# Dilated attention rows by way of DRAM, dilated tiles first in every batch, and a first batch whose low-rank product is formed in fp32

## The chip, the cores and the metric

The kernel runs on one core of a Trainium2 chip. The metric is the device time of one execution in microseconds (us), the median of several runs; smaller is better. A profiled execution has a time of its own and a span, from its first to its last instruction, and the trace gives each instruction's start and length within that span. The engines are named as in the profile: PE multiplies matrices (PEld loads its weights), DVE, ACT and POOL work on rows of elements, SP issues the transfers (SPq).

## The reference, cut to what matters

Eight batches of 576 tokens. Eight heads of width 64: the first four attend to a window of the last 32 tokens, the last four to 32 tokens spread over 128, every fourth one (dilation 4). The heads side by side give x, 576 x 512 for each batch. Then, with U (576 x 32) and V (32 x 576),

```
mask_plain = (rel >= 0) & (rel < 32)
mask_dil   = (rel >= 0) & (rel < 128) & (rel % 4 == 0)
attn = softmax(where(mask, q @ k.T / 8, -1e9))       # per head
x  = heads side by side of (attn @ v)                # (8, 576, 512)
u  = x + (x.T @ U @ V).T                             # mixes tokens, per batch
out = u + relu(u @ w_ch1) @ w_ch2                    # 512 -> 2048 -> 512
```

U, V and the two weight matrices arrive as 64-bit floating point; everything else is fp32. Below, t is U.T @ x (32 x 512 for a batch), so that V.T @ t is what is added to x.

## The kernel before, in words

**Chunks.** The 4608 tokens are 36 tiles of 128; three tiles make a chunk, and the last loop runs over twelve chunks. In a chunk, `layer1(f)` (L778) multiplies the turned rows of u by 128 columns of w_ch1 in twelve matmuls, for f from 0 to 15; ACT (L783) and DVE (L784) apply the relu and split the result into a high and a low part; `layer2(f)` (L798) multiplies by 128 rows of w_ch2 in nine matmuls. Matrices are split into a high and a low part of a rounded format (fp32r), and three products of parts stand for one fp32 product; an fp32 matmul stands in the profile as two instructions. The attention of later batches is laid into the chunks by a queue with positions, so PE works on both.

**Attention.** A batch has 18 tiles of 64 queries, nine of each kind; two tiles make a group, and there are nine groups (`NGB`). `TILES` gives their order: before, the nine plain tiles and then the dilated ones. For dilated heads the tokens are sorted by their remainder modulo 4, so that a dilated tile is 64 neighbours in that order. A group is scored (L395), masked and reduced (DVE L415), put through exp (ACT L419), turned (PE L432, copied by L434 or L436), multiplied by v (L461, tile pv) and divided by its sum (L465, L466, L489). Plain rows land in their x tile at once (L489). Dilated rows land in a tile xp, and SP copies them from there to every fourth row of x (L493), in as many transfers as `runs_of` finds.

**t and its use.** `split` (L507, L509) makes a high and a low part of half a tile's columns (c is 0 for the plain half, 1 for the dilated half); `t_mm` (L529) multiplies both by U, itself split into parts; `t_evict` (L538 to L544) takes t out of PSUM as four stacked parts of 32 rows, some by ACT and some by DVE. For most tiles `mix` (L553, L555) adds V.T @ t to x. For the three tiles of chunk 0 it is done while they are turned: `lay_x` (L563) turns x by a matmul with the identity and leaves the sum open, `lay_mix` (L570) adds the second term, `transp` (L611 on ACT, L612 on DVE) takes high and low part out. The first batch computes t of its dilated half from xp, before the rows have moved, with rows of U in that order (`us_d`).

**Weights.** Each of the 32 pieces of the two weight matrices (512 KB of 64-bit numbers) and the three pieces of U and V goes through `weight_step`, a pipeline of four stages: `fetch64` on SP (L208, L210), `narrow_a` on ACT (L217 to L219), `narrow_b` with a shift on DVE (L225) and an add on POOL (L226), and for weights `narrow_c`: the high part by ACT (L230) or DVE (L232), the low part by POOL or, for some, DVE (L233). One step advances each stage by a piece. Before, steps for U and V follow items 5 to 10 of the first batch's list, steps for the weights every third item from the eleventh (at a low priority), five more follow the list, and chunk 0 has four per f. Instructions are put in order on each engine by a scheduler that goes by priority and estimated times.

Of the kernel before, what the change touches and what calls it, by code (L numbers as in the profile page):

```python
# [10 lines left out]
F32 = mybir.dt.float32  # L11
# [37 lines left out]
TILES = [(0, j) for j in range(NJ)] + [(1, NJ - 1)] + [(1, j) for j in range(NJ - 1)]  # L49
# [6 lines left out]
PRE_AT = range(5, 11)  # L56
U_AT = 5
PRE_N = 5
W_FROM = 11
W_EACH = 3  # L60
# [4 lines left out]
XL_LAST = 3  # L65
XL_DVE = ((0, 1), (1, 1))
# [18 lines left out]
XHLS = 10  # L85
HI1 = 0.85
POST0 = 0
# [7 lines left out]
XPS = 4  # L95
# [37 lines left out]


def runs_of(b, half, j):
    out = []
    for r in range(QB):
        g = b * S + token_of(half, QB * j + r)
        t, row = divmod(g, P)
        step = 1 if half == 0 else DIL  # L140
        if out and out[-1][1] == t and row == out[-1][2] + step * out[-1][3]:
            out[-1][3] += 1
        else:
            out.append([r, t, row, 1])
    return out
# [14 lines left out]
def attention_moe_kernel(ctx: ExitStack, tc: tile.TileContext, qk1, qk2, vv, masks, wide, ident, ut, vt, w1, w2, out):  # L160
# [28 lines left out]
    signs = [const.tile([P, DM, 2], F16, name=f"sign{i}") for i in range(NSIGN)]  # L189
    NPT = 2  # L190
# [51 lines left out]
    def finish_small(kind):  # L242
        def go(v):
            if kind == "u":
                v3 = v.rearrange("p (a r) -> p a r", r=RANK)
                for dst, src in ((us, v3[:, 0:9]), (held_u[0], v3[:, 9:])):
                    nc.scalar.copy(out=dst[:, :, 0:RANK], in_=src)
                    nc.vector.tensor_tensor(out=dst[:, :, RANK:], in0=src, in1=dst[:, :, 0:RANK].bitcast(F32), op=ALU.subtract)
            else:
                cs = slice(kind * HALF_V, (kind + 1) * HALF_V)  # L250
                nc.scalar.copy(out=vs[:, cs], in_=v)
                lo = slice(3 * RANK, 4 * RANK)
                nc.vector.tensor_tensor(out=vs[lo, cs], in0=v[lo], in1=vs[lo, cs].bitcast(F32), op=ALU.subtract)
        return go

    def finish_w(f, layer, n):
        def go(v):
# [3 lines left out]
            narrow_c(v, h, l, nc.vector if n % L_ON_DVE == 0 and n >= L_FROM else nc.gpsimd, n % 4 < H_ON_ACT)  # L261
# [13 lines left out]
    def weight_step(lo, hi):  # L275
# [10 lines left out]
        if lo <= i - 1 < hi:  # L286
            n = pieces[i - 1][1]
            if 2 * F_LAST <= i - 1 - NSMALL:
# [161 lines left out]

    def weighted(g, pt):
# [5 lines left out]
        for u in range(2):  # L457
            for h in range(2):
                hs = slice(h * DV, (h + 1) * DV)
                for i in range(2):  # L460
                    nc.tensor.matmul(pv[rows[i]:rows[i] + QB, 2 * u + h, :], lhsT=pt[:, 2 * i + u, QB * h:QB * (h + 1)],  # L461
# [8 lines left out]
        for (half, j), row in zip(tiles, rows):  # L470
            if half == 0:
                dst = x_tile((b * S + j * QB) // P)[:, 0:HALF_D]
            else:
# [9 lines left out]
                moves += [(t, to, n, row + r) for r, t, to, n in runs_of(b, half, j)]  # L483
# [8 lines left out]
        for t, to, n, r in sorted(moves):  # L492
            nc.sync.dma_start(out=x_tile(t)[to:to + DIL * (n - 1) + 1:DIL, HALF_D:], in_=xp[r:r + n])  # L493
        if moves and b == 0:
            split(b, part, 1, xp, slice(QB * (2 - len(DPART[part])), P))

    t_ps = {}
    t_sb = {}
    xs = {}

    def split(b, i, c, x, rs):
        if b == 0:
            xhl = early.tile([P, 2, HALF_D], F32R, tag="xhl", name=f"xhl{b}_{i}_{c}", bufs=XHLS)
        else:
            xhl = xpool.tile([P, 2, HALF_D], F32R, tag="x", name=f"xhl{b}_{i}_{c}")
        xh, xl = xhl[:, 0], xhl[:, 1]
        nc.scalar.copy(out=xh[rs], in_=x[rs])  # L507
        eng = nc.vector if (b, c) in XL_DVE or (b == 0 and i >= XL_LAST) else nc.gpsimd
# [6 lines left out]

    def t_mm(b, i, c):
        assert 0 in finished
        parts = batch_parts(b)
        if b == 0 and c == 1:
            u = held_u[0][:, i]  # L520
            rs = slice(QB * (2 - len(DPART[i])), P)
        else:
            t, row, n, tok = parts[i]
            rs = slice(row, row + n)
            u = us[:, 8 if n < P else tok // P if tok % P == 0 else 4 + tok // P]
        if (b, c) not in t_ps:
            t_ps[b, c] = psum.tile([2 * RANK, HALF_D], F32, tag="ps", name=f"t{b}_{c}")
        for k, m in enumerate(xs.pop((b, i, c))):
            nc.tensor.matmul(  # L529
                t_ps[b, c], lhsT=u[rs], rhs=m[rs],  # L530
                start=(i == 0 and k == 0), stop=(i == len(parts) - 1 and k == 1),
            )

    def t_evict(b, c):
        ts_ = work.tile([P, HALF_D], F32R, tag="t" if b else "t0", name=f"ts{b}_{c}", bufs=1 if b else 2)
# [3 lines left out]
        nc.vector.tensor_tensor(out=ts_[r[1]], in0=tp[r[0]], in1=ts_[r[0]].bitcast(F32), op=ALU.subtract)  # L539
        if b == 0:  # L540
            nc.vector.tensor_copy(out=ts_[r[2]], in_=tp[r[1]])
        else:
            nc.scalar.copy(out=ts_[r[2]], in_=tp[r[1]])
        nc.scalar.copy(out=ts_[r[3]], in_=tp[r[0]])  # L544
# [15 lines left out]
    def lay_x(t):  # L560
        tp = psum.tile([P, KC, P], F32, tag="acc", name=f"tp{t}", bufs=CT)
        for k in range(KC):
            nc.tensor.matmul(tp[:, k, :], lhsT=x_tile(t)[:, k * P:(k + 1) * P], rhs=id_sb, start=(k == 0), stop=False)  # L563
        sums[t] = tp

    def lay_mix(t):
        tp = sums.pop(t)
        for k in range(KC):
            c, o = divmod(k, KC // 2)
            nc.tensor.matmul(tp[:, k, :], lhsT=t_sb[0, c][:, o * P:(o + 1) * P],  # L570
                             rhs=vs[:, 64 + t * P:64 + (t + 1) * P], start=False, stop=(k == KC - 1))
        return tp
# [20 lines left out]
    def transp(t):  # L593
# [7 lines left out]
        elif t in sums:  # L601
            tp = lay_mix(t)
# [9 lines left out]
        nc.vector.tensor_tensor(out=l, in0=tp, in1=h.bitcast(F32), op=ALU.subtract)  # L612

    def batch_items(b):
# [3 lines left out]
        for s in range(NGB + LAG):  # L618
# [31 lines left out]
            if b < SPLIT:  # L650
                attn.append([lambda pre=pre, units=units, post=post: (pre(), [x() for x in units], post())])
# [4 lines left out]
        for c in range(2):  # L656
            more = []
            for i in range(n + 1):
                def go(i=i, c=c):
                    if i > 0 and (b, c) != (0, 0):  # L660
                        t_mm(b, i - 1, c)
                    if i < n and (b, c) != (0, 1):
# [5 lines left out]
        first = NJ // 2 + LAG + 1 + (POST0 if b == 0 else 0)  # L668
# [13 lines left out]
        if b == 0:  # L682
            hold = after[0][n + 1:]
# [220 lines left out]
```

## Time and profile before

| | |
|---|---|
| median of 3 runs | 1010.58 us (1010.44 to 1010.71) |
| the profiled execution | 1010.63 us |
| its span | 1008.9 us |
| mean granted clock of PE | 0.987 |
| PE busy | 982.8 us |
| first `layer1` matmul of chunk 0 | 52.96 us |
| first stores of chunk 0 | 148.72 us |
| first `layer1` matmul of chunk 1 | 155.52 us |

A row of a view by groups gives line, engine, operation, output and inputs, shapes and count, then the busy time, the mean of one in ns, and the idle time of the engine ahead of them with what ended it. A row of the timeline gives start, length, engine, line and operation, and in brackets the idle time ahead and its releaser; neighbours of one form are merged. A row of the windows gives for a stretch of time the length, each engine's busy time with its instruction count, the granted clock of PE (1.00 is full), and the busy share and rate of the DMA engines. A busy PE may still run at a reduced clock.

### The profile page before, as it was taken

How to read it: one execution, taken by the hardware profiler on the slowest of the kernel's cores; microseconds unless marked ns; L12 is line 12 of the kernel's file. 1: busy time of each engine (PE TensorE's matmuls, PEld its weight loads, DVE VectorE, ACT ScalarE, POOL GpSimd, SP SyncE). 2: the span in 40 equal slices, each digit the busy share in tenths (PEclk: the TensorE clock that was granted, in tenths of full speed). 3: DMA queues.
4: the chain of work that ended last, by engine and by line, in shares of the span. 5: the costliest groups of instructions: out<-in, count | busy, mean ns of one | idle time of the engine just before them, and what ended most of it. 6: DMA issues, size and time to landing. Idle time of an engine off the chain costs nothing.

```text
span 1008.9 us, 18032 instructions
## 1 busy us (share of the span) xinstructions
PE 982.8 (97%) x5928; PEld 861.8 (85%) x5928; DVE 580.9 (58%) x1957; ACT 408.7 (41%) x985; POOL 326.9 (32%) x520
## 2 busy tenths in 40 slices
PE   6799989999999999999999999999999999999998
PEld 6688768888988889888888888888898888999997
DVE  3878787665468636676367653876547863311211
ACT  5799954443245423344244432444323542111110
POOL 0489954242135413252132430434222431000000
PEclk9699998999999999999999999999999999999999
DMA  9699534332324315243242333433232420500000
GB/s 276 182 302 313 152 111 116 88 113 82 87 78 125 94 38 145 74 121 89 67 115 77 103 91 73 124 89 111 83 87 80 122 63 24 134 1 1 32 1 32
DMA packets 96909, 103.31 MB, mean 102 GB/s; under 512 B 12816, under 2 KB 83536, under 8 KB 96816
## 3 DMA queue, kind: packets, MB, share of 16 engines
q1 hardware_dynamic: 96816, 102.16, 35.6%
q8 instruction: 48, 0.79, 0.3%
q14 instruction: 45, 0.37, 0.1%
HBM read 80.08 MB, written 17.30 MB: 97 GB/s over the span
## 4 chain that ended last, share of the span: by engine, by line
PE 86%; DVE 4%; DMA 2%; ACT 2%; POOL 2%; issue 1%; SPq 1%; DVEq 0%; ACTq 0%; POOLq 0%
PE ph L778 37%; PE acc L798 37%; PE pv L461 4%; PE s L384 3%; PE t L529 2%; PE s L395 2%; POOL v L226 1%; DMA zd<-z 1%; DMA raw<-w 1%; PE m L553 1%; DVE xhl L509 1%; PE ptp L432 1%; ACT sign L218 1%; DMA qk<-qk 1%; ACT sign L219 0%
## 5 line engine op out<-in xcount | busy, mean ns | idle before, releaser
L798 PE MATMUL acc<-w2h,hh 128*128 128x512 f32 x576 | 229.3, 398 | 3.5 <-ACT hh L783 2.2
L798 PE MATMUL acc<-w2l,hh 128*128 128x512 f32 x576 | 228.0, 396 | 0.0
L361 POOL TENSOR_TENSOR qks<-qkr,qks 128x160 fp32r<-128x160 f32 x192 | 103.2, 537 | 375.3 <-ACT qks L360 251.6
L784 DVE SCALAR_TENSOR_TENSOR hl<-ph,hh 128x384 fp32r<-128x384 f32 x192 | 106.2, 553 | 192.2 <-ACT hh L783 191.3
L798 PE MATMUL acc<-w2h,hl 128*128 128x512 f32 x576 | 211.9, 398 | 0.4 <-DVE hl L784 0.4
L783 ACT ACTIVATE hh<-ph 128x384 fp32r<-128x384 f32 x192 | 93.2, 485 | 277.1 <-PE ph L778 267.9
L778 PE MATMUL ph<-uth,w1l 128*128 128x384 f32 x768 | 175.0, 340 | 0.0
L778 PE MATMUL ph<-uth,w1h 128*128 128x384 f32 x768 | 174.6, 342 | 0.3 <-ACT uth L611 0.3
L778 PE MATMUL ph<-utl,w1h 128*128 128x384 f32 x768 | 172.6, 338 | 0.0
L419 ACT ACTIVATE p<-p,nmax 128x160 f32<-128x160 f32 (+1 forms) x288 | 110.3, 408 | 110.3 <-DVE nmax L415 109.0
L778 PEld LDWEIGHTS ph<-uth,w1h 128*128 128x128 f32 x768 | 138.7, 189 | 15.6 <-ACT uth L611 0.5
L778 PEld LDWEIGHTS ph<-uth,w1l 128*128 128x128 f32 x768 | 136.4, 189 | 1.2 <-issue 0.2
L778 PEld LDWEIGHTS ph<-utl,w1h 128*128 128x128 f32 x768 | 135.3, 188 | 1.6 <-DVE utl L612 0.2
L360 ACT CAST qks<-qkr 128x288 fp32r<-128x288 f32 x192 | 80.8, 429 | 121.8 <-PE s L384 81.4
L798 PEld LDWEIGHTS acc<-w2h,hl 128*128 128x128 f32 x576 | 107.4, 188 | 24.4 <-DVE hl L784 1.0
L798 PEld LDWEIGHTS acc<-w2h,hh 128*128 128x128 f32 x576 | 108.2, 188 | 21.2 <-ACT hh L783 3.2
L445 DVE STREAM_TRANSPOSE pt<-p 32x128 f32<-32x128 f32 x384 | 115.6, 301 | 16.7 <-ACT p L419 11.9
L798 PEld LDWEIGHTS acc<-w2l,hh 128*128 128x128 f32 x576 | 108.3, 188 | 16.1
L412 DVE TENSOR_TENSOR p<-s,wide_sb 128x160 f32<-128x160 f32 x192 | 60.0, 318 | 67.7 <-PE s L384 65.8
L364 POOL TENSOR_TENSOR qks<-qkr,qks 64x128 fp32r<-64x128 f32 x192 | 89.1, 464 | 15.0
L509 POOL TENSOR_TENSOR xhl<-x,xhl 128x256 fp32r<-128x256 f32 (+1 forms) x68 | 50.2, 759 | 83.8 <-ACT xhl L507 59.8
L384 PE MATMUL s<-qks 128*128 128x320 f32 x192 | 60.4, 320 | 2.6 <-DVE x L555 1.5
(75 smaller groups left out, 929.2 us busy)
## 6 DMA issues: line engine op xcount, KB each, us to landing
qkr<-qk SPq DMA_DIRECT2D x192, 144.0 KB, 2.2
raw<-w SPq DMA_DIRECT2D x26, 512.0 KB, 5.0
v<-vv SPq DMA_DIRECT2D x126, 97.5 KB, 2.1
out<-x SPq DMA_DIRECT2D x36, 256.0 KB, 2.3
zd<-z SPq DMA_DIRECT2D x120, 64.0 KB, 2.0
xt<-zd SPq DMA_DIRECT2D x30, 256.0 KB, 2.9
qk<-qk SPq DMA_DIRECT2D x9, 448.0 KB, 8.7
qkr<-qk SPq DMA_DIRECT2D x18, 224.0 KB, 4.9
```

The lines of the kernel that those rows point to most:

```text
L360: nc.scalar.copy(out=t[:, 0:QK2], in_=raw)
L361: nc.gpsimd.tensor_tensor(out=t[:, QK2:], in0=raw[:, P:], in1=t[:, P:QK2].bitcast(F32), op=ALU.subtract)
L364: eng.tensor_tensor(out=t[lo, 0:P], in0=raw[lo, 0:P], in1=t[lo, 0:P].bitcast(F32), op=ALU.subtract)
L384: nc.tensor.matmul(sp, lhsT=t[:, 0:P], rhs=t[:, P:], start=True, stop=True)
L412: nc.vector.tensor_tensor(out=p_sb[:, u, :], in0=sp[:, 0:KW], in1=wide_sb[:, kind], op=ALU.add)
L419: nc.scalar.activation(out=p_sb[:, u, 0:w], in_=p_sb[:, u, 0:w], func=AF.Exp, bias=nmax[:, u:u + 1], scale=-1.0,)
L445: nc.vector.transpose(out=to[:, :, WIN * (r % 2):WIN * (r % 2 + 1)], in_=p_sb[rs, :, QB * s + WIN * k:QB * s + WIN * (k + 1)])
L509: eng.tensor_tensor(out=xl[rs], in0=x[rs], in1=xh[rs].bitcast(F32), op=ALU.subtract)
L778: nc.tensor.matmul(ph, lhsT=w[:, k, :], rhs=u[:, k, :], start=(n == 0), stop=(n == len(seq) - 1))
L783: nc.scalar.activation(out=hh, in_=ph, func=AF.Relu)
L784: nc.vector.scalar_tensor_tensor(out=hl, in0=ph, scalar=0.0, in1=hh.bitcast(F32), op0=ALU.max, op1=ALU.subtract)
L798: nc.tensor.matmul(acc[i], lhsT=h[:, ss], rhs=w, start=(c > 0 and f == 0 and n == 0), stop=(f == FC - 1 and n == 2))
```

## The change

1. `TILES` has the dilated tiles first, in all batches; the middle group holds the last tile of each kind, the last four groups are plain. For batches from the second on, the dilated half's `split`, `t_mm`, `t_evict` and `mix` now go with the last attention groups, and the plain half's come after them (`for c in (1, 0)`).
2. Dilated rows no longer go from xp straight to x. Each of the five groups with dilated tiles writes its rows in one transfer to a DRAM tile `dil_rows` in their sorted order; at the middle group five reads (one for each x tile that the batch touches) bring them to x in token order. `runs_of` is gone.
3. In the first batch `split` is gone: `t_first` multiplies U in fp32 by x (or xp) in fp32, one matmul for each of the ten parts, spread over the groups as their rows are ready. `t_evict` leaves out the low-U part there (its rows in a tile `t0s` are zeroed once). `us_d` is gone; U is kept as fp32 (`u32`).
4. `lay_x` and `lay_mix` work on one half at a time. The plain half of `lay_x` is put among the last items, the dilated half behind the last pv matmul; `lay_mix` of the dilated half comes ahead of the split of the plain half's t.
5. Steps for U and V follow items 3 to 8; three weight steps follow items 8 to 10; the next five steps stand behind the plain half's `t_evict` (`issue_after` orders instructions on the ACT and DVE queues behind that copy and that subtraction). The other steps stay in chunk 0, four per f. The high part of the first six weight pieces is made by ACT. One mask is loaded one group earlier.

```
-TILES = [(0, j) for j in range(NJ)] + [(1, NJ - 1)] + [(1, j) for j in range(NJ - 1)]
+TILES = [(1, j) for j in range(NJ)] + [(0, NJ - 1)] + [(0, j) for j in range(NJ - 1)]
...
-PRE_AT = range(5, 11)
+PRE_AT = range(3, 9)
-W_FROM = 11
-W_EACH = 3
+W_AT = range(8, 11)
-XL_LAST = 3
-XL_DVE = ((0, 1), (1, 1))
+H_FIRST = 9
+XL_DVE = ((1, 0),)
...
+t0s = [const.tile([P, HALF_D], F32R, name=f"t0_{c}") for c in range(2)]
+for e in t0s:
+    nc.gpsimd.memset(e[2 * RANK:3 * RANK].bitcast(F32), 0.0)
...
-for t, to, n, r in sorted(moves):
-    nc.sync.dma_start(out=x_tile(t)[to:to + DIL * (n - 1) + 1:DIL, HALF_D:], in_=xp[r:r + n])
+if moves:
+    (at_, r), n = moves[0], QB * len(moves)
+    nc.sync.dma_start(out=dil_rows[b].rearrange("r q e -> (r q) e")[at_:at_ + n], in_=xp[r:r + n])
+if moves and g % NGB == ODD:
+    rows_ = dil_rows.pop(b)
+    for t, row, n, tok in batch_parts(b):
+        nc.sync.dma_start(out=x_tile(t)[row:row + n, HALF_D:],
+                          in_=rows_[:, tok // DIL:(tok + n) // DIL].rearrange("r q e -> q r e"))
 if moves and b == 0:
-    split(b, part, 1, xp, slice(QB * (2 - len(DPART[part])), P))
+    xps[part] = xp
...
+def t_first(i, c):
+    if c == 0:
+        t, row, n, tok = batch_parts(0)[i]
+        rs = slice(row, row + n)
+        k = 8 if n < P else tok // P
+        m = x_tile(t)[:, 0:HALF_D]
+    else:
+        rs = slice(QB * (2 - len(DPART[i])), P)
+        k = 9 + i
+        m = xps.pop(i)
+    ...
+    nc.tensor.matmul(t_ps[0, c], lhsT=held_u[0][rs, k * RANK:(k + 2) * RANK], rhs=m[rs],
+                     start=new, stop=(i == (0 if c else len(DPART) - 2)))
...
-if b == 0:
-    nc.vector.tensor_copy(out=ts_[r[2]], in_=tp[r[1]])
-else:
+if b > 0:
     nc.scalar.copy(out=ts_[r[2]], in_=tp[r[1]])
...
+def first_of(g):
+    if g <= ODD:
+        t_first((g + 1) % len(DPART), 1)
+    if g == ODD:
+        t_evict(0, 1)
+    if g >= ODD:
+        t_first((g - ODD - 1) % len(DPART), 0)
...
+if b == 0 and g + LAG + 1 == NGB + LAG - 1:
+    with tc.issue_after(last_pv[NGB - 1].ins):
+        for t in range(CT):
+            lay_x(t, 1)
...
-after[1] = sums0 + [hold[0]] + after[1][:m] + lays + [after[1][m]] + turns + mixes
+after = [[], [lambda: first_of(NGB - 1)] + lays + [after[1][n + 1]] + turns + mixes]
...
-for _ in range(PRE_N):
-    weight_step(NSMALL, NPIECE)
+with tc.issue_after(held_t[0].ins), tc.issue_after(held_t[1].ins):
+    for _ in range(PRE_N):
+        weight_step(NSMALL, NPIECE)
```

More of the change, by code (lines that the diff above doesn't have):

```diff
@@ L94 @@
 QKS = 9
-XPS = 4
+XPS = 5
 DVE_FROM = 2
@@ L132, in row_of @@
     return QB * (j % 2) if j < NJ - 1 else QB * (1 - b % 2)
[L135 to L142, printed above, removed]
-        else:
-            out.append([r, t, row, 1])
-    return out
 def batch_parts(b):
@@ L449, in turn @@
         return pt
+    last_pv = {}
+    dil_rows = {}
     def weighted(g, pt):
@@ L482, in weighted @@
                 dst = xp
-                moves += [(t, to, n, row + r) for r, t, to, n in runs_of(b, half, j)]
+                if b not in dil_rows:
+                    dil_rows[b] = dram.tile([DIL, RES, HALF_D], F32, tag="xd", name=f"xd{b}", bufs=2)
+                moves.append((QB * j, row))
             parts.append((dst, row, half))
@@ L530, in t_mm @@
                 t_ps[b, c], lhsT=u[rs], rhs=m[rs],
-                start=(i == 0 and k == 0), stop=(i == len(parts) - 1 and k == 1),
+                start=(i == 0 and k == 0), stop=(i == len(batch_parts(b)) - 1 and k == 1),
             )
     def t_evict(b, c):
-        ts_ = work.tile([P, HALF_D], F32R, tag="t" if b else "t0", name=f"ts{b}_{c}", bufs=1 if b else 2)
+        ts_ = t0s[c] if b == 0 else work.tile([P, HALF_D], F32R, tag="t", name=f"ts{b}_{c}", bufs=1)
         r = [slice(i * RANK, (i + 1) * RANK) for i in range(4)]
@@ L558, in attention_moe_kernel, with lay_x, lay_mix @@
     sums = {}
[L560 to L569, printed above, removed]
+    def lay_x(t, c):
+        if c == 0:
+            sums[t] = psum.tile([P, KC, P], F32, tag="acc", name=f"tp{t}", bufs=CT)
+        for k in range(c * KC // 2, (c + 1) * KC // 2):
+            nc.tensor.matmul(sums[t][:, k, :], lhsT=x_tile(t)[:, k * P:(k + 1) * P], rhs=id_sb, start=(k == 0), stop=False)
+    def lay_mix(t, c):
+        tp = sums[t]
+        for k in range(c * KC // 2, (c + 1) * KC // 2):
+            o = k % (KC // 2)
             nc.tensor.matmul(tp[:, k, :], lhsT=t_sb[0, c][:, o * P:(o + 1) * P],
-                             rhs=vs[:, 64 + t * P:64 + (t + 1) * P], start=False, stop=(k == KC - 1))
-        return tp
+                             rhs=vs[:, 64 + t * P:64 + (t + 1) * P], start=False, stop=(c == 0 and k == KC // 2 - 1))
     def add_mix(t, acc):
@@ L601, in transp @@
         elif t in sums:
-            tp = lay_mix(t)
+            lay_mix(t, 0)
+            tp = sums.pop(t)
         else:
@@ L655, in batch_items @@
         after = []
-        for c in range(2):
+        for c in (1, 0):
             more = []
@@ L699, in attention_moe_kernel @@
     early = early_open.enter_context(tc.tile_pool(name="early", bufs=1))
-    held_u.append(early.tile([P, len(DPART), 2 * RANK], F32R, name="us_d"))
+    held_u.append(early.tile([P, (NU + 1) * RANK], F32, name="u32"))
+    nc.gpsimd.memset(held_u[0][:, NU * RANK:], 0.0)
     for g in range(NGB):
```

71 lines of the change are left out of this document (35 added, 36 removed).

## The prediction

> **What bounds the kernel now.** I read the page first, then the windows cut at the stages, then the timeline of the gaps.
>
> ```profile
> span 1008.9 us, 18032 instructions
> PE   6799989999999999999999999999999999999998
> PEclk9699998999999999999999999999999999999999
> ```
>
> ```profile
> 31.00:53.00 22.00, 16.66 (x97) 13.26 (x93) 16.84 (x44) 16.63 (x39) 11.72 (x11) 0.61 0.54 167
> 53.00:124.00 71.00, 70.39 (x491) 60.91 (x491) 55.88 (x155) 68.36 (x147) 65.39 (x51) 1.00 0.80 253
> 124.00:148.30 24.30, 21.57 (x119) 17.48 (x118) 18.78 (x33) 14.80 (x41) 15.20 (x14) 1.00 0.35 102
> 148.30:155.50 7.20, 3.89 (x19) 2.54 (x18) 6.61 (x22) 4.36 (x10) 3.74 (x8) 0.82 0.80 230
> 155.50:160.00 4.50, 4.50 (x16) 4.50 (x16) 3.56 (x14) 1.18 (x3) 1.15 (x3) 0.53 0.59 146
> 160.00:1009.00 849.00, 842.66 (x4962) 743.12 (x4960) 465.56 (x1599) 284.31 (x697) 226.43 (x428) 1.00 0.29 80
> ```
>
> In each row of the windows stand PE, PEld, DVE, ACT and POOL busy, then the granted clock. From 160 us on PE works 842.66 of 849.00 us at full clock: nothing that reorders other engines gains there, and the change adds no PE work there. What can be gained lies ahead: 22 us in which PE runs 97 matmuls at clock 0.61 (the tail of the first batch), chunk 0 itself, in which PE, ACT and POOL are all nearly full (70.39, 68.36 and 65.39 of 71), and a gap of 7.2 us before chunk 1, followed by 4.5 us at clock 0.53.
>
> The timeline of the first stage:
>
> ```profile
> 27.30 0.43 DVE L489 TENSOR_TENSOR xp<-pv,ssum 64x256 f32<-64x256 f32 x1
> 27.45 0.52 ACT L217 ACTIVATE v<-raw 128x352 f32<-128x352 f32 x1 [0.66 <-DMA raw<-vt]
> 31.31 1.14 ACT L419 ACTIVATE p<-p,nmax 128x96 f32<-128x96 f32 x4
> 31.93 14.14 SPq L493 DMA_DIRECT2D x<-xp  x21
> 33.68 1.13 PE L461 MATMUL pv<-v,pt 96*64 96x65 f32 x16 [0.86 <-DVE pt L436]
> 37.45 0.42 DVE L489 TENSOR_TENSOR xp<-pv,ssum 128x256 f32<-128x256 f32 x1
> 40.89 1.48 DVE L509 TENSOR_TENSOR xhl<-xp,xhl 128x256 fp32r<-128x256 f32 x1
> 42.43 0.48 PE L529 MATMUL t<-xhl,us_d 128*64 128x256 f32 x1 [1.54 <-DVE xhl L509]
> 42.94 0.36 ACT L538 CAST ts<-t 32x256 fp32r<-32x256 f32 x1 [1.29 <-PE t L529]
> 45.39 0.36 ACT L544 CAST ts<-t 32x256 fp32r<-32x256 f32 x1
> 46.17 0.53 SPq L210 DMA_DIRECT2D raw<-w  x1
> 52.34 0.57 ACT L611 CAST uth<-tp 128x512 fp32r<-128x512 f32 x1
> 52.56 1.29 POOL L226 TENSOR_TENSOR v<-v,sign 128x512 int32<-128x512 int32 x1 [5.39 <-ACT sign L219]
> 52.81 0.67 ACT L217 ACTIVATE v<-raw 128x512 f32<-128x512 f32 x1
> 52.96 0.96 PE L778 MATMUL ph<-uth,w1h 128*128 128x384 f32 x4 [0.26 <-ACT uth L611]
> ```
>
> The last pv ends at 33.68 + 1.13 = 34.81 us, chunk 0 begins at 52.96: 18.15 us between. Two chains fill them. One: the last xp is made late (37.45) and its split ends at 42.37, since DVE has splits and weight shifts ahead of it; t is out at 45.75. The other: SP issues 21 transfers for 14.14 us, so the next weight transfer leaves only at 46.17, ACT's next weight piece follows, and POOL has nothing for 5.39 us before 52.56.
>
> **The change part by part.** First, t of the first batch. Removed: ten splits, ACT and DVE or POOL one operation each. After the last pv there remain sum, reciprocal and the multiplication on DVE: between 34.81 and the end of the last xp (37.87) lay 3.06 us with other work between; with that work gone I take 1.2. Then one fp32 matmul of 256 columns.
>
> ```profile
> L395 PE MATMUL s<-qk 128*128 128x96 f32 x72 | 12.7, 329 | 7.9 <-DMA qk<-qk 5.7 <-DVE x L489 1.6 <-DVE ssum L466 0.5
> L570 PE MATMUL tp<-vs,ts 128*128 128x128 f32 x12 | 3.1, 409 | 0.0
> ```
>
> No fp32 matmul of that shape is in the trace. The 36 fp32 products of 96 columns took 12.7 us, 0.35 each, so by columns 256/96 x 0.35 = 0.94; the two half-clock matmuls of 0.48 that it stands for (42.43 above) come to the same. I take 1.2, with 0.7 to 1.9 for the range. PE sits half idle there, so only the last of the ten counts. Then copy, subtraction and copy: 0.36 each for the copies (42.94 and 45.39 above), the subtraction of the same 32 x 256 about as long, 1.2 us with the handing over. The split of t is done at 34.81 + 1.2 + 1.2 + 1.2 = 38.4. Besides, ACT held the last group's exp until 31.31 behind six narrowings of V that began at 27.45; the change moves V's steps two items up, but V lands when it did, since its transfer waits in a full queue. I count 0.9 for what the lighter ACT and DVE give: **split of t done at 37.5** (34.5 to 42). The open sum of the plain half of the turn is ahead of it; what is left is half a `lay_mix` for the first tile (two of the four matmuls of L570, 3.1/12 each, 0.5) and three copies of 0.57 on ACT (52.34): first `layer1` at 37.5 + 0.6 + 1.8 = 39.9, against 52.96: 13 us earlier for PE.
>
> Second, what of this reaches chunk 0's end. There the weights decide, not PE:
>
> ```profile
> L218 ACT ACTIVATE sign<-raw 128x512 f16<-128x512 f32 (+1 forms) x34 | 23.3, 686 | 0.8 <-POOL v L226 0.8
> L219 ACT ACTIVATE sign<-raw 128x512 int16<-128x512 uint32 (+1 forms) x34 | 22.8, 671 | 0.0
> L217 ACT ACTIVATE v<-raw 128x512 f32<-128x512 f32 (+1 forms) x34 | 18.8, 583 | 2.4 <-DMA raw<-w 1.7 <-POOL w2l L233 0.6
> L230 ACT CAST w1h<-v 128x512 fp32r<-128x512 f32 x7 | 4.3, 613 | 0.0
> L226 POOL TENSOR_TENSOR v<-v,sign 128x512 int32<-128x512 int32 x29 | 41.1, 1424 | 7.8 <-ACT sign L219 6.3 <-DVE w1h L232 0.7 <-DVE ssum L466 0.4
> 137.96 1.48 POOL L233 TENSOR_TENSOR w1l<-v,w1h 128x512 fp32r<-128x512 f32 x1 [0.41 <-ACT w1h L230]
> 139.73 0.33 PE L778 MATMUL ph<-uth,w1h 128*128 128x384 f32 x1
> ```
>
> The last `layer1` starts at 139.73, 0.29 us after its weights are done on POOL (139.44). From 52.56 on POOL works through them with few breaks. So the end moves by as much as ACT and POOL reach the same state earlier. POOL: at 52.56 it begins the add of the fourth piece. After the change it begins the first low part 0.6 after t's split, at 38.1, and has five operations to do (three low parts, two adds): 5 x 1.4 = 7.0, so 45.1: **7.5 us earlier**. ACT: at 52.81 it begins the fifth piece. After the change, from 37.5: two pieces of the three passes of L217 to L219 (2 x 1.94, here 3.8), three high parts (1.8, as L230), two more copies of the turn (1.2), and three high parts taken over from DVE (1.8) make 8.6, so 46.1: 6.7 earlier; the 1.7 us in which ACT waited for a weight transfer behind L493 can come back, which makes 8.4. I take 7.5, between these; the weight transfers themselves are not held (the ordering binds ACT and DVE only), and SP no longer has 21 moves ahead of them. What is given up at zero: the ten DRAM transfers. SP drops the moves
>
> ```profile
> x<-xp SPq DMA_DIRECT2D x88, 32.0 KB, 1.9
> zd<-z SPq DMA_DIRECT2D x120, 64.0 KB, 2.0
> xt<-zd SPq DMA_DIRECT2D x30, 256.0 KB, 2.9
> qk<-qk SPq DMA_DIRECT2D x9, 448.0 KB, 8.7
> ```
>
> and a hop now lands after 2.0 + 2.9 = 4.9 us by the like rows of the DRAM turn, against 1.9. The middle group's xp was ready at 27.73, so the rows are in x by about 35, hidden behind the four plain groups; without that cover it would be 3 us on the path. SP now waits for the middle group's write before the reads, and behind them stand the fetches for batch 1 and the weight transfers: 2.0 and five issues of about 0.6 (3.05/5 below) are 5 us in place of 14.14, so SP is free sooner. Later batches have their four plain groups as the same cover, at zero.
>
> Third, the gap before chunk 1. It costs 7.20 - 3.89 = 3.3 us idle and 4.5 x 0.47 = 2.1 us of clock, 5.4 in all.
>
> ```profile
> 133.86 3.05 SPq L493 DMA_DIRECT2D x<-spare  x5
> 141.55 0.67 PE L529 MATMUL t<-xhl,us 128*64 128x256 f32 x3 [0.49 <-DVE xhl L509]
> 150.04 0.42 PE L384 MATMUL s<-qks 128*128 128x320 f32 x1 [1.46 <-DVE x L555]
> ```
>
> Batch 1's last half waits for 3.05 us of issues and a landing of 1.9; after the change the late half is the plain one, in x at once. But the wait that ends at 150.04 is for the last addition of a mix on DVE, and how early PE takes the mixes among `layer2`'s matmuls is open, so part of that may gain nothing: I take 2.0 of 5.4 (0 to 5.4).
>
> Sum against the profiled execution (1010.63, which is 0.05 above the median): 1010.63 - 7.5 - 2.0 = **1001.1 us**.
>
> **The rivals.** PE-bound: weights keep pace after all. POOL's 7.8 us ahead of L226 and ACT's 2.4 are for it, the 0.29 us between last weights and last `layer1` against. Then 13.0 less the half-clock start as at 155.50 (2.1), 2.0 at the gap, and up to 3.3 of idle PE in chunk 0: 994.4 to 997.7, say 996. Here a rule bears on the price: the granted clock is 0.61 in 31 to 53 and 0.53 for 4.5 us after the gap. The Trainium skill, TensorE: Matmul & The Clock Gate, "What's actually happening", has an idle window of about 3.4 us halve the clock and a busy one restore it; by that the start would lose an estimated 1.7 in place of 2.1.
>
> Less: t's split at 41, as V's narrowing still delays the last exp and the DVE stays crowded; ACT's account then gives 52.8 - 41 - 8.6 = 3.2, the gap 1: 1006.4.
>
> Slower: the dilated rows return late. The dilated half of `lay_x` stands on PE behind the last pv and ahead of the last plain t matmul; PE takes its work in order, so if the rows are missing, t waits, and with it ACT's and DVE's weight steps from the fourth on, which in the old order ran beside it. The DMA rows for it: with the queue full, qk took 8.7. Two such legs with 2.5 of issues end at 27.73 + 8.7 + 2.5 + 8.7 = 47.6; plus 2.4 for t and its split, 50. Chunk 0 would end 50 + 8.6 - 52.8 = 5.8 later: 1016. It decides from 44.2 on, where ACT's account is zero. Against it: small SBUF rows took 1.9. The Trainium skill, DMA: Bandwidth & Descriptors, "Latency and other measured facts", gives HBM access 0.2 us on average and 2 at high load, inside a fixed cost of about 2; by that an estimated 27.73 + 2 x 3.8 + 2.5 = 37.8, too early to do harm, and no run here shows it yet.
>
> No change: t's split near 43 to 44, the gap as it was: 1010.
>
> **How the numbers follow.** A difference of 0.2% (2 us) is about what a measurement of this kernel can tell. Forecast 0.58 (own range 998 to 1004.5), PE-bound 0.15, less 0.15, no change 0.04, slower 0.08. Faster is 0.58 + 0.15 + 0.15 = 0.88, same 0.04, slower 0.08. The range 994.5 to 1007 takes in PE-bound and less and leaves out the last two cases and the ends.
>
> **What would show it.** Right: SP has five writes and five reads where L493 stood; no L507 or L509 before chunk 0; t's split done by 36 to 40 and the first ph at 38 to 43; the last w1l on POOL near 132 and still within 1 us of its `layer1`; chunk 1's first ph at 145 to 147. Wrong: idle time of PE at L563 put down to a DMA from dil_rows, a first weight low part after 44, ph stalls on weights at f of 1 to 4 longer than 6 us in all, or PE idle after 160 us.

## The result, and the profile after

The kernel after took 1003.82 us (median of six runs, 1002.63 to 1008.14), the kernel before 1010.53 in the same series (six runs, 1009.84 to 1011.81). The ratio is 0.9946, 95% interval 0.9929 to 0.9963: faster by about 0.5%. The profiled execution of the kernel after is the slowest of its six, 1008.14 us; the other five lie between 1002.63 and 1005.00. That difference lies at the start, as far as the profiles tell, so the start is read below from several profiles and not from this one alone.

The page of the kernel after, the span, PE and the clock:

```profile
span 1006.1 us, 17820 instructions
PE   7889999999999999999999999999999999999998
PEclk9899998999999999999999999999999999999999
```

Its windows at the stages of the prediction (length, then PE, PEld, DVE, ACT and POOL busy, then the granted clock, the DMA share and rate):

```profile
31.00:53.00 22.00, 15.76 (x120) 11.76 (x118) 12.91 (x38) 15.39 (x33) 9.57 (x8) 0.84 0.80 251
53.00:124.00 71.00, 69.06 (x477) 60.58 (x478) 53.38 (x149) 66.56 (x142) 63.11 (x52) 0.98 0.81 257
149.30:156.87 7.57, 4.27 (x19) 2.84 (x17) 6.89 (x23) 4.41 (x11) 3.54 (x8) 0.74 0.74 212
156.87:160.00 3.13, 3.13 (x10) 3.13 (x11) 3.04 (x12) 1.04 (x3) 1.38 (x3) 0.53 0.66 170
160.00:1006.00 846.00, 841.47 (x4967) 745.47 (x4965) 465.32 (x1600) 286.04 (x697) 228.72 (x428) 1.00 0.31 85
```

The start is no shorter here: PE works 15.76 us of 22 at clock 0.84, where before it was 16.66 at 0.61, and the gap before chunk 1, which now begins at 156.87, is still there, with a clock of about half behind it up to 160 us. The timeline shows why:

```profile
29.27 0.53 ACT L204 ACTIVATE v<-raw 128x352 f32<-128x352 f32 x1 [1.47 <-DMA raw<-vt]
32.72 1.60 SPq L488 DMA_DIRECT2D xd<-xp  x3
37.23 0.36 ACT L552 CAST t<-t 32x256 fp32r<-32x256 f32 x1
37.64 1.13 PE L453 MATMUL pv<-v,pt 96*64 96x65 f32 x16 [2.23 <-ACT t L552]
39.77 3.15 SPq L492 DMA_DIRECT2D x<-xd  x5
40.76 1.07 PE L453 MATMUL pv<-v,pt 96*64 96x65 f32 x14
44.79 0.52 PEld L572 LDWEIGHTS tp<-id_sb,x 128*128 128x128 f32 x4 [0.39 <-DMA x<-xd]
45.74 0.36 ACT L552 CAST t<-t 32x256 fp32r<-32x256 f32 x1 [0.48 <-DVE t L549]
46.31 1.29 POOL L213 TENSOR_TENSOR v<-v,sign 128x512 int32<-128x512 int32 x1 [7.76 <-DVE v L212]
49.07 0.56 ACT L619 CAST uth<-tp 128x512 fp32r<-128x512 f32 x1
142.03 0.86 PE L803 MATMUL ph<-uth,w1h 128*128 128x384 f32 x4
151.20 0.41 PE L373 MATMUL s<-qks 128*128 128x320 f32 x1 [1.64 <-DVE x L563]
```

The last pv ends at 40.76 + 1.07 = 41.83 us, 7.0 later than before. V lands later still (its first narrowing starts at 29.27), and there is a wait that the trace of the old kernel does not have: the pv of a group needs a free PSUM buffer (PSUM is where the kernel has the products of PE written), one of them holds t of the dilated half, and the copy that empties it (L552, 37.23) stands in ACT's queue behind a weight piece; PE waits 2.23 us for it. The split of the plain half's t is out at 45.74 + 0.36 = 46.10 (45.75 before). The first `layer1` of chunk 0 starts at 53.97 (52.96 before), the last at 142.03 (139.73).

So in this profile everything up to chunk 1 is a little later than before, and the execution is still 2.5 us shorter. The gain is where I had forecast none. The windows of both kernels from the end of chunk 1 (its first x<-acc, L823 and L848) to the end of the span, before and after:

```profile
240.50:1008.86 768.36, 762.16 (x4439) 672.52 (x4437) 410.50 (x1386) 250.37 (x612) 196.23 (x369) 1.00 0.29 79
```

```profile
241.71:1006.08 764.37, 759.75 (x4436) 673.83 (x4434) 410.59 (x1386) 249.93 (x607) 194.22 (x364) 1.00 0.30 83
```

4.0 us, of which PE's idle time gives 1.6 (6.20 to 4.62) and its busy time 2.4, with the same matmuls (4439 and 4436 records) at full clock in both. PE's busy time is what the profile counts; the ends of matmuls are modelled there, so the sum of both is surer than the shares. I call this stretch the late part and what lies ahead of it the start.

### The profile page after: what moved, and what is told of

The parts are those of the page before. It is cut to its first block, busy times and chain, and to the rows that moved or that the text cites. A ratio compares the mean times of both kernels' runs of the same rounds, so it can differ in the third digit from the quotient of the medians.

```text
span 1006.1 us, 17820 instructions
## 1 busy us (share of the span) xinstructions
PE 982.9 (98%) x5928; PEld 865.1 (86%) x5928; DVE 575.4 (57%) x1944; ACT 407.9 (41%) x977; POOL 326.1 (32%) x520
## 4 chain that ended last, share of the span: by engine, by line
PE 88%; DMA 4%; DVE 2%; ACT 2%; POOL 1%; issue 1%; SPq 0%; DVEq 0%; POOLq 0%; ACTq 0%
PE ph L803 39%; PE acc L823 38%; PE pv L453 4%; PE s L373 3%; DMA v<-vv 2%; PE t L539 2%; DMA raw<-vt 1%; DMA raw<-w 1%; PE m L561 1%; PE s L384 1%; POOL v L213 1%; ACT sign L205 1%; ACT sign L206 0%; DVE v L212 0%; DMA qkr<-qk 0%
## 5 line engine op out<-in xcount | busy, mean ns | idle before, releaser
L823 PE MATMUL acc<-w2h,hh 128*128 128x512 f32 x576 | 229.1, 398 | 0.0
L823 PE MATMUL acc<-w2l,hh 128*128 128x512 f32 x576 | 228.3, 396 | 0.0
L823 PE MATMUL acc<-w2h,hl 128*128 128x512 f32 x576 | 213.5, 397 | 0.0
L803 PE MATMUL ph<-uth,w1l 128*128 128x384 f32 x768 | 172.4, 340 | 0.2 <-POOL w1l L220 0.2
L823 PEld LDWEIGHTS acc<-w2h,hl 128*128 128x128 f32 x576 | 107.7, 188 | 23.6
L823 PEld LDWEIGHTS acc<-w2h,hh 128*128 128x128 f32 x576 | 108.2, 188 | 16.5 <-ACT hh L808 0.2
L823 PEld LDWEIGHTS acc<-w2l,hh 128*128 128x128 f32 x576 | 108.3, 188 | 15.8
L453 PEld LDWEIGHTS pv<-v,pt 96*64 96x64 f32 x1152 | 42.2, 141 | 25.1 <-issue 8.9
```

Of the source, the lines that this page charges most:

```text
L453: last_pv[g] = nc.tensor.matmul(pv[rows[i]:rows[i] + QB, 2 * u + h, :], lhsT=pt[:, 2 * i + u, QB * h:QB * (h + 1)], rhs=loaded[g, 1, i][:, ...
L803: nc.tensor.matmul(ph, lhsT=w[:, k, :], rhs=u[:, k, :], start=(n == 0), stop=(n == len(seq) - 1))
L823: nc.tensor.matmul(acc[i], lhsT=h[:, ss], rhs=w, start=(c > 0 and f == 0 and n == 0), stop=(f == FC - 1 and n == 2))
```

## The experiments

All times on the chip are medians, with the kernel before run beside them. The last column is the late part, from the profile of each; it repeats to 0.1 us between three profiles of the kernel after, while the start varies by several us from run to run. (The kernel after: 1001.81 to 1008.53 in twelve runs of the first group.) The three profiled executions of the kernel after took 1008.14, 1008.53 and 1006.85 us, all well over the medians of their series (1003.82, 1005.27 and 1004.46), while most of the other profiles lie near or under theirs. So the columns of the start show the kernel after later than is usual for it, and a comparison of starts from one profile each is worth little. "Split of t" is the end of the last operation, on ACT or DVE, that takes the plain half's t out of PSUM in the first batch; "last layer1" is the first matmul of the last `layer1` of chunk 0.

| kernel | time | before | ratio, 95% | split of t | first ph | last layer1 | chunk 1's first ph | late part |
|---|---|---|---|---|---|---|---|---|
| before (profile) | | | | 45.75 | 52.96 | 139.73 | 155.52 | 768.4 |
| after (profile) | | | | 46.10 | 53.97 | 142.03 | 156.87 | 764.4 |
| after, repeated | 1005.27 | 1009.95 | 0.9956 (0.9939 to 0.9972) | 45.62 | 54.43 | 142.55 | 157.46 | 764.4 |
| V's steps late | 1006.61 | 1009.95 | 0.9975 (0.9954 to 0.9995) | 47.38 | 52.12 | 142.91 | 159.75 | 764.3 |
| late batches moved directly | 1004.79 | 1009.95 | 0.9959 (0.9939 to 0.9979) | 40.86 | 49.40 | 136.84 | 151.75 | 765.5 |
| weight steps free | 1003.26 | 1009.95 | 0.9947 (0.9929 to 0.9965) | 47.02 | 53.19 | 139.03 | 151.56 | 764.8 |
| before, late order new | 1008.28 | 1010.58 | 0.9976 (0.9961 to 0.9991) | 45.38 | 51.76 | 137.72 | 154.02 | 765.4 |
| after, late order old | 1009.72 | 1010.58 | 0.9991 (0.9976 to 1.0006) | 43.27 | 51.69 | 139.90 | 154.78 | 769.3 |
| t copied out at once | 1006.85 | 1010.58 | 0.9969 (0.9953 to 0.9986) | 43.39 | 48.02 | 138.57 | 156.07 | 764.4 |
| three start edits | 1008.02 | 1010.58 | 0.9977 (0.9962 to 0.9993) | 45.82 | 51.71 | 140.88 | 155.34 | 764.8 |
| before, t together | 1011.45 (one run) | 1011.28 | | 47.41 | 54.46 | 140.45 | 157.20 | 767.9 |
| before, all late edits | 1007.08 | 1011.28 | 0.9967 (0.9953 to 0.9980) | 44.80 | 51.74 | 137.80 | 154.44 | 765.0 |
| after, third time | 1004.46 | 1011.28 | 0.9945 (0.9924 to 0.9966) | 45.19 | 53.04 | 139.83 | 154.71 | 764.4 |
| weight steps free, t together | 1002.74 | 1011.28 | 0.9929 (0.9910 to 0.9948) | 48.36 | 54.56 | 139.69 | 152.53 | 763.6 |

**The kernel after, repeated**, as the partner of the next three.

> The changed kernel once more, to see which of its stages vary from run to run. If the start (the loads of the first batch) is what varies, this profile has the first layer-1 matmul of chunk 0 several us earlier than 53.97, and the span shorter by about as much, with 849 us from the first layer-1 matmul of chunk 1 to the end as before. If the start does not vary, it is again near 54 and the time is near 1008. Time by the six runs so far: 1002.6 to 1005, once 1008.1.

1005.27 us. The same kernel lies at 0.9946, 0.9956 and 0.9945 of the kernel before in its three series.

**The theory of the start: V's narrowing.** V's two pieces wait until the last group's exp:

```
-PRE_AT = range(3, 9)
+PRE_AT = range(3, 7)
+V_AT = range(7, 12)
...
+if i in V_AT:
+    with ExitStack() as order:
+        if i > V_AT[0]:
+            order.enter_context(tc.issue_after(last_exp[0].ins))
+        weight_step(1, NSMALL)
```

> V's narrowing steps are put behind the last exp of the first batch on ACT; the rest is the changed kernel. Theory: V's passes stand in ACT's and DVE's queues ahead of the last group's exp and hold the tail of the first batch back. Then the last pv ends near 37 instead of 41.8, the split of the plain half's t is done near 42 instead of 46.1, and the time falls by 2 to 4 us against the changed kernel (to about 1000.5). Rival: chunk 0's end is set by the weight work of ACT and POOL alone, which V's place does not change; then the tail moves but the last low part of w_ch1 on POOL stays near 141.9 and the time is within 1 us of the changed kernel.

1006.61 us, no gain over the repeat. The theory's own signs failed too: the last pv ended at 42.38 and not near 37, since the wait for the PSUM buffer was there again (2.42 us), and the split was done at 47.38 and not near 42. The last low part of w_ch1 ended at 142.35, near the rival's 141.9. The first ph came 2.3 us earlier than in the repeat, but chunk 0 took 107.6 us from there to chunk 1's first ph instead of 103.0. V's narrowing ahead of the last exp is seen in the timeline; that it costs time overall is not borne out.

**The route in the late batches.** Batches 2 to 7 move their dilated rows directly, as before; the order of the tiles stays new:

```
+if b >= SPLIT:
+    direct += [(t, to, n, row + r) for r, t, to, n in runs_of(b, half, j)]
...
+for t, to, n, r in sorted(direct):
+    nc.sync.dma_start(out=x_tile(t)[to:to + DIL * (n - 1) + 1:DIL, HALF_D:], in_=xp[r:r + n])
```

> Batches 2 to 7 copy their dilated rows straight from xp to x again, as in the kernel before (batches 0 and 1 by DRAM, tile order as changed). From the first layer-1 matmul of chunk 1 to the end it took 853.4 us before and 849.2 after. Theory: fewer issues on SP give these 4 us; then this kernel takes 3 to 4 us more than the changed one, all of it behind 157 us. Rival: the order of the tiles gives them (the late half no longer waits for moves); then it is within 1 us of the changed kernel.

1004.79 us. Its window of the late part:

```profile
236.20:1001.70 765.50, 760.86 (x4439) 674.23 (x4437) 412.18 (x1386) 248.57 (x607) 195.39 (x364) 1.00 0.29 79
```

765.5 against 764.4, and 850 us from chunk 1's first ph to the end, as the rival had it: the way through DRAM is worth about 1 us of the 4.0 here, the rest stays without it.

**The weight steps.** They no longer wait for t's split:

```
-with tc.issue_after(held_t[0].ins), tc.issue_after(held_t[1].ins):
-    for _ in range(PRE_N):
-        weight_step(NSMALL, NPIECE)
+for _ in range(PRE_N):
+    weight_step(NSMALL, NPIECE)
```

> The weight steps from the fourth on are not put behind the split of t; the rest is the changed kernel. Theory: weights and t use the same ACT, so what t loses the weights gain: first layer-1 matmul 1 to 3 us later, POOL's first low part as much earlier, time within 1.5 us of the changed kernel. Rival: without the order the weights' passes stand ahead of the split of t and chunk 0 starts 4 us or more later, and the time rises by 3 us or more.

1003.26 us, 2.0 under the repeat, with overlapping intervals; the profiled execution of the repeat (1008.53) is the longest of its twelve, this one (1003.25) lies at its median. From first ph to chunk 1's first ph, in the repeat and here:

```profile
54.43:157.46 103.03, 97.40 (x623) 83.27 (x622) 78.33 (x206) 86.74 (x197) 81.34 (x71) 0.96 0.66 204
```

```profile
53.19:151.56 98.37, 94.43 (x627) 82.40 (x627) 79.86 (x203) 79.86 (x186) 74.28 (x65) 0.98 0.65 201
```

POOL's first low part is at 37.98 us instead of 47.54 in the profile of the kernel after, so ACT and POOL have 7 us of weight work less left in chunk 0 (86.74 to 79.86, 81.34 to 74.28) and the chunk is 4.7 us shorter, although t's split came later (47.02). The kernel before has its first low part at 40.71, so in that profile the change has the weights start 7 us later than before. Without it they run ahead: POOL's last low part of w_ch1 ends at 129.22, ten us before the last `layer1` (139.03), where in the kernel after it ends at 141.87, 0.16 us before it. That freeing the weights gains time overall is likely, not settled.

**The order of the tiles, alone and undone.** First the kernel before with the new order in batches 2 to 7 only (the halves of t change places with it), everything else as before; second the kernel after with the old order there, in which the rows are read back from DRAM after the last group:

```
+LATE = [(1, j) for j in range(NJ)] + [(0, NJ - 1)] + [(0, j) for j in range(NJ - 1)]
...
-        return TILES[2 * (g % NGB) + u // 2]
+        return (TILES if g < SPLIT * NGB else LATE)[2 * (g % NGB) + u // 2]
...
-        for c in range(2):
+        for c in (0, 1) if b < SPLIT else (1, 0):
```

```
+LATE = [(0, j) for j in range(NJ)] + [(1, NJ - 1)] + [(1, j) for j in range(NJ - 1)]
...
-        if moves and g % NGB == ODD:
+        if moves and g % NGB == (ODD if b < SPLIT else NGB - 1):
...
-        for c in (1, 0):
+        for c in (1, 0) if b < SPLIT else (0, 1):
```

> The kernel before, with the dilated tiles first (and the dilated half's t, split and mix ahead of the plain half's) in batches 2 to 7 alone; rows still go straight from xp to x, batches 0 and 1 and all weight steps as before. Theory: the order of the tiles in the late batches gives the 4 us that the changed kernel gains behind chunk 1's first layer-1 matmul; then this kernel needs 849 to 850 us from there to the end in place of 853.4, and its time is 3.5 to 4.5 us under that of before. Rival: those 4 us come with the start's changes or are chance of the order of instructions; then it needs 853 us and its time is that of before within 1 us.

> The changed kernel with the plain tiles first again in batches 2 to 7 (rows by DRAM, read back after the last group). Theory (order of the tiles): 852.5 to 854 us from chunk 1's first layer-1 matmul to the end, time 3 to 4.5 us over the changed kernel. Rival (the DRAM path or the start gives them): 849 to 850 us, time as the changed kernel within 1 us.

The windows of the late part of the one and of the other:

```profile
239.10:1004.50 765.40, 760.77 (x4439) 674.35 (x4437) 412.15 (x1386) 247.77 (x607) 194.26 (x364) 1.00 0.29 79
```

```profile
238.80:1008.10 769.30, 762.50 (x4439) 671.96 (x4437) 408.95 (x1386) 252.86 (x612) 197.08 (x369) 1.00 0.30 83
```

The order alone takes 3.0 us from the kernel before, 1.6 of idle time (6.20 to 4.63) and 1.4 of busy time (762.16 to 760.77); undone, it gives back 4.9 to the kernel after. From chunk 1's first ph to the end the two took 850.5 and 853.3 us: the second is what the theory of the order forecast, the first half a us over it. Of the nine kernels with dilated tiles first in the late batches eight, whatever their start, lie at 764.3 to 765.5 and the ninth (the last of the table) at 763.6; the three with plain tiles first lie at 767.9 to 769.3. The times agree in sign: 2.3 us under the kernel before for the order alone (3.5 to 4.5 were expected), and only 0.9 left when it is undone. The route through DRAM adds to it, by 1.1 us in the kernel after and by 0.4 in the kernel before (765.4 to 765.0, the kernel with all late edits below).

**The theory of the start: the held PSUM buffer, and all three edits.** In the first, the second high copy of the first batch's t is issued right behind the first, ahead of the subtraction; the second kernel has this, V's steps late and the weight steps free.

```
+        again = nc.scalar.copy(out=ts_[r[3]], in_=tp[r[0]]) if b == 0 else None
         low = nc.vector.tensor_tensor(out=ts_[r[1]], in0=tp[r[0]], in1=ts_[r[0]].bitcast(F32), op=ALU.subtract)
```

> The changed kernel; in the first batch's split of t the second copy of the high part is issued right behind the first, so that ACT does not take weight passes in between and PSUM is free sooner. Theory: the pv of the eighth group no longer waits for that copy (2.2 us in the profile); the split of the plain half's t, then the weights from the fourth step on, come 2 to 3 us earlier against the first score of the last group, and the time falls by 1.5 to 3 us. Rival: the loads of the start decide, and pv waits for something else as late; then the interval from the last group's score to chunk 1's first layer-1 matmul stays 128 to 130 us.

> The changed kernel with three edits: V's narrowing behind the last exp, the copies of t's split next to each other, and the weight steps from the fourth on not held behind the split of t. Theory: weights start 8 us sooner than in the changed kernel (POOL's first low part near 38) while t loses little; interval from the last group's score to chunk 1's first layer-1 matmul 124 to 126 us, time 2 to 4 us under the changed kernel. Rival: the three edits only move the same ACT work around; interval 128 us, time as the changed kernel within 1.5 us.

1006.85 and 1008.02 us: nothing gained over the kernel after. In the first the wait went as meant: its timeline has the eighth group's pv at 34.08 without it. The second high copy ends at 40.90, but the subtraction on DVE stands behind an addition that waits 3.62 us for rows from DRAM, so the split is done only at 43.39. The waits of PE in chunk 0 show what came later:

```profile
34.08 0.69 PE L453 MATMUL pv<-v,pt 96*64 96x65 f32 x16
42.53 0.42 DVE L565 TENSOR_TENSOR x<-x,m 128x256 f32<-128x256 f32 x1 [3.62 <-DMA x<-xd]
42.98 0.41 DVE L550 TENSOR_TENSOR t<-t,t 32x256 fp32r<-32x256 f32 x1
```

```profile
PE pv L453 <- DMA v<-vv: 3.2, 3, 1.6
PE m L563 <- DVE x L565: 1.6, 1, 1.6
```

The split came 2.7 us before that of the kernel after in its first profile, and 1.8 before its third. The first ph came at 48.02, six us before; the last `layer1` at 138.57, 3.5 us before; chunk 1's first ph still at 156.07, 128.5 us behind the last group's score, as the rival had it. So chunk 0 gave nearly all of it back: PE waited 3.2 us for loads of v for batch 1 ahead of the last `layer1` (0.8 in the kernel after), and from there to chunk 1 it took 17.5 us in place of 14.8.

**Is it the scatter of t's matmuls?** In the late part t's ten matmuls of a half stand closer together after the change. One half from the timeline of tile t, before and after (the span of its starts stands behind the three durations):

```profile
L529 PE MATMUL t<-xhl,us x10: 277/280/327, 243.5 to 249.2; 128*64 128x256 f32 x8, 64*64 64x256 f32 x2
```

```profile
L539 PE MATMUL t<-xhl,us x10: 276/277/328, 242.4 to 244.7; 128*64 128x256 f32 x8, 64*64 64x256 f32 x2
```

Counted as unbroken series in the order of PE's starts, they stand in 51 runs before and in 32 after from 160 us on (the expectation below counts rows of the timeline, which gives 53). The next kernel is the one before with t's matmuls of the second half put behind that half's splits:

```
+if b >= SPLIT and c == 1:
+    if i < n:
+        split_x(b, i, c)
+    else:
+        for e in range(n):
+            t_mm(b, e, c)
+    return
```

> The kernel before, with one edit: in batches 2 to 7 the ten t matmuls of the second half (the dilated one) stand together behind that half's five splits, where the kernel before puts each pair behind its own split. It tells what of the late batches' gain is the scatter of these matmuls over PE's queue. Measure: the time from the first x<-acc of chunk 1 to the end of the span (768.4 us in the kernel before, 764.4 in the kernel after, 765.4 in the kernel before with dilated tiles first in the late batches). If the scatter is the mechanism (53 runs of t matmuls from 160 us on before, 32 after; 25.5 us busy before, 22.3 after): 764.5 to 766.0, and t's rows busy 22 to 23. If it is the order of the tiles itself (which half's rows come last, and what the splits and evictions then wait for): 767.5 to 769.0, whatever t's rows show. Between: both.

The late part is 767.9 us, which looks like the second answer, but t's rows are those of the kernel before (18.7 and 6.8 us busy) and its matmuls still stand in 51 runs:

```profile
L529 PE MATMUL t<-xhl,us 128*64 128x256 f32 x96 | 18.7, 283 | 0.0
L529 PE MATMUL t<-xhl,us 64*64 64x256 f32 x24 | 6.8, 317 | 0.0
```

The scheduler took them apart again. The edit did not make what it should test, so it decides nothing.

**The start against the late part, and a version with both findings.** Three kernels on one chip: the kernel before with all late edits of the change (order and DRAM route from batch 2 on, as in the kernels above); the kernel after; and the kernel after with the weight steps free and t's matmuls of both halves together in the late batches.

> The kernel before in its first two batches (tiles, moves, t of batch 0, weight steps all as before), and the kernel after in batches 2 to 7: dilated tiles first, the dilated half's t first, dilated rows through DRAM. Beside a repeat of the kernel after on the same chip it parts the late batches' gain from the start's. If the late batches carry most of the gain: 4.0 us under the kernel before (764.0 to 765.0 from chunk 1's first x<-acc to the end), so 0.9960, and the kernel after lies 0.5 to 2.5 us under it. If the start carries what I forecast for it (9.5 us): the kernel after lies over 5 us under it.

> The kernel after once more, as the partner of the run with only its late batches and of the version with both halves' t together. Expected 0.9935 to 0.9965 of the kernel before, and 764.4 us from chunk 1's first x<-acc to the end. By the theory of the late batches 0.5 to 2.5 us under the kernel that has only the late edits; by the forecast's theory of the start over 5 us under it.

> The kernel after with two edits: the weight steps from the fourth on no longer wait for t's split, and in batches 2 to 7 the t matmuls of either half stand together behind the half's splits. If the scatter of t costs in the first half too (five runs over 7.3 us in chunk 1): 763 to 764 from chunk 1's first x<-acc to the end against 764.4, and the time 1 to 3 us under the kernel after on the same chip, most of it from the weights (chunk 1's first ph at 151 to 153 us). If neither edit is worth anything: within 1 us of the kernel after, 764.2 to 765.0 in the late part.

The late edits alone come to 1007.08 (twelve runs), the whole change to 1004.46 (six): 4.2 us of 6.8 by the late part, 2.6 by the start, from medians of runs that spread over 5 us each. The last kernel has the lowest median of all, 1002.74, 1.7 under the kernel after. Its window of the late part and t's rows there:

```profile
236.80:1000.40 763.60, 759.00 (x4439) 674.61 (x4437) 410.33 (x1388) 249.51 (x607) 195.15 (x364) 1.00 0.29 83
```

```profile
L539 PE MATMUL t<-xhl,us 128*64 128x256 f32 x96 | 14.8, 285 | 0.0
L539 PE MATMUL t<-xhl,us 64*64 64x256 f32 x24 | 6.0, 309 | 0.0
```

Here the scheduler did keep them closer, 21 runs instead of 32, and the late part is 0.8 us shorter, as much as PE's busy time (759.75 to 759.00). Its nearer partner, the kernel with the weight steps free alone, has 30 runs, 759.73 us busy and 764.8. Over all profiles fewer runs go with less busy time: 762.0 to 762.5 us at 51 runs, 760.8 and 760.9 at 36 (the two kernels with the new order and without the DRAM route), 759.7 to 759.9 at 30 to 32, 759.0 at 21. Its first ph is the latest in the table (54.56) and chunk 1's first ph is among the earliest (152.53), as with free weight steps alone. The intervals of this kernel and of the kernel after overlap, so the 1.7 us are likely, not settled.

## Why the prediction was right, and where it was wrong

Sign, range and the likeliest case held: 1001.1 forecast, 1003.82 measured, with the profiled execution at 1008.14. The sum behind it did not. I had 7.5 + 2.0 = 9.5 us from the start and zero from the late part; the runs give about 2.6 and 4. That the two errors partly cancel, so that the total came inside the range, is luck. Of the signs that I had named, the five writes and five reads and the last low part of w_ch1 within 1 us of its `layer1` came true (though at 141.87 and not near 132); the first low part at 47.54 (over 44), the first ph at 53.97 (38 to 43) and chunk 1's first ph at 156.87 (145 to 147) said wrong.

**"From 160 us on ... nothing that reorders other engines gains there."** This step failed most. A PE busy for 842.66 of 849.00 us was taken for a bound. Of the 4.0 us, 1.6 are idle time, and the waits of PE from 240 us on in the kernel before name nearly all of it; in the kernel after, and in the kernel before with the new order alone, that view is empty:

```profile
PE acc L798 <- DVE x L823: 1.1, 1, 1.1
PE s L384 <- DVE nmax L415: 0.2, 1, 0.2
PE s L384 <- DVE x L489: 0.2, 1, 0.2
```

The other 2.4 are busy time: the same matmuls take less when they follow one another differently. That the order of the tiles gives the idle time and 1.4 of the busy time is shown by the two kernels that differ in it alone; the remaining 1.0 comes with the route through DRAM. By which pairs of matmuls is not shown: at the rate of the last kernel against its nearer partner (0.73 us for nine runs of t fewer), 51 to 32 runs would be worth an estimated 1.5 of the 2.4.

**"Split of t done at 37.5."** 46.10 here, 45.62 and 45.19 in the repeats, 40.86 to 48.36 in the other kernels with the new start. The lowest, 40.86, is of a kernel whose first two batches are those of the kernel after, in an execution of 1003.54 us; so part of the delay belongs to the long executions that were profiled. The step from the last pv to the split was about right (3.6 taken, 41.83 to 46.10 is 4.3); the last pv itself was carried over from the old trace at 34.81, as if the order of the tiles, the new matmuls among them and a PSUM buffer in use could not move it. The price of the fp32 matmul was right. In the rows of t, each matmul is two instructions:

```profile
L528 PE MATMUL t<-x,u 128*64 128x256 f32 x8 | 3.5, 524 | 0.0
L528 PE MATMUL t<-xp,u 128*64 128x256 f32 x8 | 1.9, 379 | 0.0
```

0.76 to 1.05 us each, for 0.94 worked out and 1.2 taken.

**"First `layer1`" 2.4 us behind the split.** 7.9 in the profile of the kernel after (7.2 before): the three copies of the turn on ACT (the first at 49.07) stand between passes of weight pieces, the very steps that were put behind the split. They are only a part of it: with the weight steps free it is still 6.2.

**Chunk 0 follows the weights, and these follow t's split (7.5 us).** This account held for the last `layer1`; what failed was the time of the split that went into it. By the account the last `layer1` starts 139.73 + 8.6 - 52.8 = 95.5 us behind the split. In the seven profiles with the new start in which the weight steps wait for the split, it starts 94.6 to 96.9 us behind it, with splits from 40.86 to 47.38. An execution with early loads has all of this earlier, so the agreement alone proves little; but where the weight steps are free the tie is loosened, the weights are done 7 to 10 us ahead of the last `layer1`, and with a split at 47.02 and 48.36 it starts 92.0 and 91.3 us behind (95.1 in the kernel with all three edits). So the split, 8.6 us later than forecast, left nothing of the 7.5 us in the profile of the kernel after: the last `layer1` was 2.3 us later than before, 1.9 by the account. Weights started earlier did shorten the way from first ph to chunk 1's first ph in the two kernels in which nothing else was changed at the start (98.4 and 98.0 us, against 101.7 to 103.0 in the kernel after), and did not in the kernel with all three edits (103.6). What sets the 12.5 to 17.5 us from the last `layer1` to chunk 1's first ph stays open.

**The DRAM hop at zero.** The cover held in the kernel after, the price did not. The rows of the transfers from 24 to 48 us:

```profile
xd<-xp SPq DMA_DIRECT2D x4, 128.0 KB, 6.5
x<-xd SPq DMA_DIRECT2D x4, 128.0 KB, 4.3
```

10.8 us for the two legs, where the rows of the uncrowded turn gave 4.9, and the reads leave only from 39.77 on, since the last three writes leave from 32.72 on. The rows were there at 44.79 and not at 35, past the point (44.2) from which the rival that ends slower was to decide. PE's weight load waited only 0.39 us for them, since PE was late for other reasons, and the last matmul of t (44.22) stands ahead of that load, so t did not wait. That rival's transfers came true and its consequence did not, here; in the kernel with t copied out at once t did wait, though on another engine: DVE stood 3.62 us for these rows with the subtraction of t behind. The Trainium skill, DMA: Bandwidth & Descriptors, "Latency and other measured facts", puts the fixed cost of a transfer at about 2 us, mostly memory latency that reaches 2 under load; 6.5 from issue to landing for a write of 128 KB, with its wait among full queues, is beyond that, and the estimate worked out from it in the prediction, 37.8 for the return, was seven us too early.

**The gap before chunk 1 (2.0 us).** Nothing came of it: 7.57 us with 4.27 busy, so 3.30 idle, and clock 0.53 behind it, against 7.20 with 3.89, 3.31 and 0.53. The wait that I had named as uncertain, for the last addition of a mix on DVE, stands there again at 151.20, 1.64 us instead of 1.46.

## What to carry to other kernels

A PE that is over 99% busy can still give half a percent: busy rows don't show whether the same matmuls would take less in another order, so compare the length of the same stretch under another order before calling it a bound. A time forecast along a chain should not carry a start point over from the old trace when the change touches the engine that makes it; here that was 7 of the 8.6 us by which the key step was late in the profile. A step is done when the last of its operations is, on whichever engine: in the kernel with t copied out at once the copies ended at 40.90 and the subtraction only at 43.39. And an ordering that holds work back until a critical step is done should be tried without it: here the held weight steps came back ahead of the next critical copies.

## What the runs showed of the hardware

The times of one kernel spread over 5 to 8 us in most series, while its late part differed by less than 0.1 us between three profiles; so the spread is put down to the start. The mean rate of the DMA engines over the first 40 us differs too, here in the first two profiles of the kernel after:

```profile
DMA packets 5955, 11.15 MB, mean 279 GB/s; under 512 B 615, under 2 KB 3317, under 8 KB 5951
```

```profile
DMA packets 6454, 11.70 MB, mean 293 GB/s; under 512 B 638, under 2 KB 3794, under 8 KB 6450
```

It does not tell the start by itself: the first ph came at 53.97 with 279 GB/s, at 54.43 with 293 and, in the third profile, at 53.04 with 296. What makes the start differ was not tried. For a stretch that is fed by loads one profile is no measure, and a gain of a few us there needs a dozen runs of both kernels.
